# RWKV attention on TensorE tiles of 64: weights of 48 columns instead of 64 in three products, with the PSUM rows between zeroed once

## The chip, the cores and the metric

The kernel runs on one core of a Trainium2 chip. The metric is the device time of the core in microseconds. Three runs of the kernel before took 606.13, 604.15 and 604.02 us; the median is 604.15.

The engines are named as the profile names them: PE is TensorE's product, PEld its load of the stationary operand (the weights), DVE is VectorE, ACT is ScalarE, POOL is GpSimd, and SP issues most transfers.

## The reference

An RWKV attention over batch 4, 8 heads, 768 steps and head size 48 feeds a dense block with 3072 tokens, 384 inputs and 2048 hidden units, all in float32.

```python
for t in range(S):
    cur = einsum('bhd,bhe->bhde', u * k[t], v[t])
    y[t] = einsum('bhd,bhde->bhe', r[t], state + cur)
    state = w * state + einsum('bhd,bhe->bhde', k[t], v[t])
x = y.transpose(0, 2, 1, 3).reshape(B * S, H * D)
h = x @ w_in
out = (h - tanh(h)) @ w_out
```

## The kernel before

The attention is done in chunks. A unit, of which there are 24, is one chunk of `SHORT` = 64 steps for two of the four batches: `z` counts the batch in the unit, and the two batches lie in partitions 0 to 63 and 64 to 127. Heads come in pairs: `p` counts the four pairs and `i` the head of a pair. A head has 48 numbers, but in the padded tiles each head has `PAD` = 64 places, of which the last 16 hold zeros (`padded`, L533). `HEAD[i]` is the 48 used partitions that begin at 64 i, and `HALF[z]` the 64 of a batch.

In one unit TensorE does these steps, all through `put` (L696, which the profile records as L697) except the transpositions:

- `turn` (L740, recorded as L742) transposes `r` and `k` of the unit, 128 by 128.
- `from_state` (L786) multiplies the scaled `r` with the state from earlier chunks, into `y_ps`. The weights are the state, 48 rows by 64 columns, and 64 steps move. It is left out in the first chunk.
- `levels` (L797) makes the scores of the 64 steps among themselves; VectorE then copies the masked part of them over `at` (recorded at L896).
- `outputs` (L809) multiplies the scores with `v` and adds the result to `y_ps`. The weights are `v`, 64 rows by 64 columns.
- `to_state` (L823) makes the new state's product into `kv_ps`. The weights are the scaled `k`, 64 rows by 64 columns, and the 48 columns of `v` move. It is left out in the last chunk.

Each of `from_state`, `outputs` and `to_state` has 16 puts, four over each of the four 64x64 tiles of the array[...]. A float32 product leaves two loads and two products in the trace, so a call has 32 records of each.

In units 0 and 1 (`direct`, where the block of the output `j` is 0) `outputs` has 12 puts on `v` and 12 on `extra`, which holds the last two heads split over columns 48 to 63.

`y_ps` and `kv_ps` are parts of one PSUM tile of two banks, `yk_ps` (L558). ScalarE copies `y_ps` to `xt` and `rest` (`to_xt` L842, `to_rest` L847), all 64 rows of a head with them; afterwards GpSimd's small transfers (`fill`, recorded as L854) write the last two heads from `rest` into rows 48 to 63 of `xt`. VectorE adds `kv_ps` to the state over all 128 partitions (`keep`, L857) and then multiplies by the decay. From unit 16 on (`two`) the transposed `r` and `k` and the scores stand in `yk_ps` as well.

The dense block (`Dense`) works on tiles of 256 hidden units by 256 tokens: the first product (L167), five activations on ScalarE, four operations on VectorE, and the second product (L205, or L255 with seven products in place of eight).

The order of the work on every engine comes from `Plan` (L299). Each piece of work is added with an engine, a cost written as a constant, what it comes after and a due time; `order` (L442) lays it out with these and many random variations, and the instructions are then issued in that order. Work that is issued directly, such as the memsets at the top of `near` (L494), is not part of the plan and stands ahead of it. At the start `w` and `u` come as eight rows, which are transposed into `cols_ps`, eight columns of `yk_ps`.

Of the kernel before, what the change touches and what calls it, by code (L numbers as in the profile page):

```python
# [11 lines left out]
F32 = mybir.dt.float32  # L12
# [20 lines left out]
PAD = 64  # L33
# [460 lines left out]
def near(ctx, tc, r, k, v, w, u, out, shared, moe_w_in, moe_w_out):  # L494
# [3 lines left out]
    V, A, T, G, Q = nc.vector, nc.scalar, nc.tensor, nc.gpsimd, nc.sync  # L498
    d = shared["dims"]
    H, D, NP, NK, B, HEAD = d.H, d.D, d.NP, d.NK, d.B, d.HEAD  # L500
# [6 lines left out]
    ps_a = ctx.enter_context(tc.tile_pool(name="n_ps_a", bufs=1, space=PSUM))  # L507
# [4 lines left out]
    def fixed(name, shape, dt=F32):  # L512
        return const.tile(shape, dt, name=name, tag=name)
# [6 lines left out]
    HALF = [slice(z * SHORT, (z + 1) * SHORT) for z in range(2)]  # L520


    rows = fixed("rows", [2 * NP, 2, PAD])
    V.memset(rows, 1.0)
    same = fixed("same", [128, SHORT])
# [3 lines left out]
    V.memset(by[:, :, 0:1], 0.0)  # L529
    V.memset(plus, 0.0)  # L530
    V.memset(plus[:, :, 0:1], 1.0)

    def padded(name, count, new=fixed):  # L533

        tiles = [new(f"{name}{i}", [128, H, PAD]) for i in range(count)]
        for t in tiles:
            G.memset(t[:, :, D:], 0.0)
        return tiles
# [16 lines left out]
    before = before.bitcast(I32)[:, None, None, :].to_broadcast([128, 2, NP, SHORT])  # L555


    yk_ps = ps_a.tile([128, 2, 512], F32, name="yk_ps", tag="yk_ps")  # L558
    banks_now = [ExitStack(), ExitStack()]

    def banks(at, name, shapes):
# [34 lines left out]
    y_ps = yk_ps[:, :, :256].rearrange("e z (p t) -> e z p t", p=NP)  # L596
    kv_ps = yk_ps[:, :, 256 : 256 + NP * D].rearrange("d z (p e) -> d z p e", p=NP)
# [98 lines left out]
    def put(*args, **how):  # L696
        T.matmul(*args, skip_group_check=True, **how)  # L697
# [3 lines left out]
    def unit(n):  # L701
# [6 lines left out]
        t = SimpleNamespace(at=ats[n % 2])  # L708
        rt, vt, kw, state = rts[n % (AHEAD + 1)], vts[n % (AHEAD + 1)], kws[n % 2], states[half]
# [13 lines left out]
        direct = j == 0  # L723

        def fetch(name, src, after):
            def run(z):
                if name == "k" and not hasattr(t, "kt"):
                    t.kt = first_k[slot] if direct else load.tile([128, H, D], F32, name="kt", tag="kt")
                to = {"r": rt, "v": vt}.get(name)
                Q.dma_start(out=(t.kt if to is None else to)[HALF[z], :, :D],  # L730
                            in_=src[half * 2 + z, :, steps_at, :].rearrange("h t d -> t h d"))

            of = [add("SP", .65, lambda z=z: run(z), after, data=.71) for z in range(2)]
            return add("none", 0, lambda: None, of)
# [5 lines left out]
        def turn(src, to):  # L740
            for p in range(NP):
                T.transpose(to[:, p * C : (p + 1) * C], src[:, 2 * p : 2 * p + 2, :].rearrange("t h d -> t (h d)"), ident)  # L742
# [34 lines left out]
                    for i in range(2):  # L777
                        put(own_lev[HALF[z], i, p], t.kU[HEAD[i], p, z], t.rT[HEAD[i], p, z], start=True, stop=True)

        def to(i, z):  # L780


            i = i ^ z if swap else i
            return slice(i * PAD, (i + 1) * PAD)

        def from_state():  # L786
            for p in range(NP if ch else 0):
                for z in range(2):
                    for i in range(2):
                        put(y_ps[to(i, z), z, p], state[HEAD[i], z, p], t.rT[HEAD[i], p, z],  # L790
                            start=p == 0, stop=False)

        def between():
# [3 lines left out]
        def levels():  # L797
            if not two:
                from_state()
            for p in range(NP):  # L800
                for z in range(2):
                    for i in range(2):
                        put(lev[HALF[z], i, p], t.kT[HEAD[i], p, z], t.rT[HEAD[i], p, z], start=not two, stop=True)
# [3 lines left out]
            G.tensor_copy(extra[slot][:, :, :, D:], vt[:, 2 * NK :, :D].rearrange("s i (k x) -> s i k x", k=NK))  # L807

        def outputs():  # L809
            for p in range(NP - direct):  # L810
                for i in range(2):
                    for z in range(2):
                        put(y_ps[to(i, z), z, p], vt[HALF[z], 2 * p + i], t.at[HALF[z], i, p],
                            start=p == 0 and not ch, stop=p == NP - 1)
            for p in range(NK if direct else 0):
                for i in range(2):
                    for z in range(2):
                        put(y_ps[to(i, z), z, p], extra[slot][HALF[z], i, p], t.at[HALF[z], i, NK],
                            start=False, stop=p == NK - 1)
            if not direct:  # L820
                to_state()

        def to_state():  # L823
            for p in range(NP if more else 0):
                for i in range(2):
                    for z in range(2):
                        put(kv_ps[i * PAD : (i + 1) * PAD, z, p], kw[HALF[z], 2 * p + i], vt[HALF[z], 2 * p + i, :D],
                            start=p == 0 or not two, stop=True)

        def given(out, y):  # L830
# [60 lines left out]
        if two:  # L891
            now = add("PE", .68, from_state, both + [x.rT, b1.xt, b1.rest, b1.add, b2.decay, x.kT], steps=64)
            begun = [add("ACT", .15, between, [now])]
        x.lev = add("PE", .7 if two else (1.35 if swap else 1.75) if ch else .7, levels,
                    begun + [x.kT, x.rT, b2.out] + ([b2.decay, b1.xt, b1.rest, b1.add] if ch else []), steps=128 if ch and not two else 64)
        x.cp = add("DVE", .64, lambda: V.copy_predicated(t.at, before, lev), [x.lev, b2.out] + ([] if product else [x.diag]))  # L896
        x.out = now = add("PE", .95 if direct else 1.3, outputs,
                          [x.cp, x.diag, x.v, b1.xt, b1.rest, b1.add] + ([x.extra] if direct else [x.kw]), steps=96 if direct else 128)
        if direct:
            now = x.out = add("PE", .6, to_state, [now, x.kw], steps=64)  # L900
# [364 lines left out]
def kernel(  # L1265
# [29 lines left out]
    with tc.manual_schedule():  # L1295
        near(tc, r, k, v, w, u, out, shared, moe_w_in, moe_w_out)
# [39 lines left out]
```

## Time and profile before

| | us |
|---|---|
| median of three runs | 604.15 |
| the profiled execution, as timed | 606.31 |
| its span in the trace | 604.5 |
| PE busy | 583.7 |
| DVE busy | 466.9 |
| ACT busy | 403.6 |
| POOL busy | 204.6 |
| L697 alone, PE busy, 0 to 40 us | 8.77 |
| L697 alone, PE busy, 40 to 230 us | 27.71 |
| L697 alone, PE busy, 230 to 340 us | 0 |
| L697 alone, PE busy, 340 to 545 us | 20.54 |

A row of a group gives the line, the engine, the operation, output<-inputs by name, for PE the rows*columns of the weights, the shape of the moving operand, and the count; then the busy time, the mean length of one in ns, the idle time before it and what ended that. A row in order of time gives start and length in us first. A row of one tile or line gives least, median and longest duration in ns, then the first and last start. Products overlap on PE, and the ends of the products are modelled, so the lengths of single ones don't add up to the time they take together. The mean clock that TensorE was granted over the span was 0.993 of full speed.

### The profile page before, as it was taken

The numbers are of one execution on the slowest core, as the hardware profiler recorded it, in microseconds if no ns is written. First come the engines' busy times: TensorE is split into PE (matmuls) and PEld (weight loads), VectorE is DVE, ScalarE is ACT, GpSimd is POOL, SyncE is SP. The second block draws the span as 40 slices with busy tenths as digits, with TensorE's granted clock in tenths as the row PEclk, the third lists the DMA queues.
The fourth block names the chain that finished last, engine by engine and source line by source line (L and its number), as shares of the span: only waits on it lengthen the run. The fifth ranks groups of instructions, "written<-read, shape, count | busy, mean of one in ns | idle before, by whom it ended". The sixth has DMA issues, their size and how long they took to land.

```text
span 604.5 us, 14282 instructions
## 1 busy us (share of the span) xinstructions
PE 583.7 (97%) x5597; PEld 493.8 (82%) x5597; DVE 466.9 (77%) x775; ACT 403.6 (67%) x902; POOL 204.6 (34%) x372
## 2 busy tenths in 40 slices
PE   7889998999999999999999999999999999999994
PEld 5556776777777689899999999888989988899993
DVE  5789989999999999987667856756986665744753
ACT  3677988899986575656666655757784757665551
POOL 5001222301000244554455443432552434453531
PEclk9989999999999999999999999999999999999998
DMA  6986569572621210111011120131310100100101
GB/s 125 185 160 116 97 120 217 112 159 73 125 60 19 48 28 11 30 26 27 2 27 27 29 44 1 35 57 26 65 25 11 41 1 9 27 7 3 26 2 31
DMA packets 86325, 33.77 MB, mean 56 GB/s; under 512 B 78536, under 2 KB 80680, under 8 KB 86248
## 3 DMA queue, kind: packets, MB, share of 16 engines
q1 hardware_dynamic: 81084, 25.57, 21.5%
q0 software_dynamic: 4992, 6.99, 5.2%
q8 instruction: 46, 0.75, 0.6%
q14 instruction: 31, 0.25, 0.1%
q10 hardware_dynamic: 172, 0.20, 0.1%
HBM read 26.94 MB, written 4.72 MB: 52 GB/s over the span
## 4 chain that ended last, share of the span: by engine, by line
PE 81%; DVE 8%; ACT 5%; issue 2%; SPq 1%; DMA 1%; POOL 0%; ACTq 0%; DVEq 0%; POOLq 0%
PE h L167 38%; PE p L255 25%; PE o L205 9%; PE yk_ps L697 6%; DMA st<-in_moe_w_in_dram 1%; PE x_ps L742 1%; DVE rT L746 1%; SPq L730 1%; ACT kT L755 1%; PE yk_ps L742 1%; DVE tg L193 1%; PE x_ps L697 1%; ACT xt L833 1%; ACT s L176 1%; DVE tg L195 1%
## 5 line engine op out<-in xcount | busy, mean ns | idle before, releaser
L167 PE MATMUL h<-xt,w_in_sb 128*128 128x256 f32 x1152 | 283.8, 383 | 2.9 <-issue 1.6
L167 PEld LDWEIGHTS h<-xt,w_in_sb 128*128 128x128 f32 x1152 | 213.7, 191 | 33.8 <-issue 3.0
L240 POOL TENSOR_TENSOR sg<-g 128x256 f32<-128x256 f32 x71 | 54.8, 772 | 178.4 <-DVE g L197 149.7
L191 DVE TENSOR_TENSOR g<-h,th 128x512 f32<-128x512 f32 x96 | 66.0, 688 | 50.8 <-ACT s L176 24.0
L255 PE MATMUL p<-mixed,sg 128*128 128x192 f32 x426 | 104.1, 326 | 0.2 <-issue 0.2
L193 DVE SCALAR_TENSOR_TENSOR tg<-s,tg 128x512 f32<-128x512 f32 x96 | 69.5, 724 | 30.7 <-ACT tg L180 16.9
L178 ACT ACTIVATE th<-h 128x512 f32<-128x512 f32 x96 | 57.4, 597 | 51.8 <-PE h L167 51.8
L180 ACT ACTIVATE tg<-h 128x512 f32<-128x512 f32 x96 | 57.1, 595 | 42.6 <-PE h L167 42.5
L176 ACT ACTIVATE s<-h 128x512 f32<-128x512 f32 x96 | 57.4, 598 | 41.1 <-PE h L167 40.8
L854 POOL DMA_DIRECT2D xt<-rest x66 | 32.2, 494 | 148.4 <-ACT rest L833 147.6
L255 PEld LDWEIGHTS p<-mixed,sg 128*128 128x128 f32 x426 | 75.0, 190 | 0.4 <-issue 0.4
L197 DVE COPY_PREDICATED g<-small,tg 128x512 f32<-128x512 int32 x96 | 71.7, 747 | 4.5
L255 PE MATMUL p<-w_out_sb,g 128*128 128x192 f32 x284 | 70.7, 331 | 0.1
L195 DVE SCALAR_TENSOR_TENSOR tg<-q,tg 128x512 f32<-128x512 f32 x96 | 67.2, 700 | 4.1 <-DVE tg L193 0.5
L182 ACT ACTIVATE q<-s,m1b 128x512 f32<-128x512 f32 x96 | 69.7, 726 | 0.7
L184 ACT ACTIVATE small<-s,smallb 128x512 f32<-128x512 f32 x96 | 69.5, 724 | 0.4
L205 PE MATMUL o<-w_out_sb,g 128*128 128x384 f32 x192 | 69.6, 488 | 0.0
L255 PEld LDWEIGHTS p<-w_out_sb,g 128*128 128x128 f32 x284 | 52.0, 190 | 7.4 <-DVE e L283 0.5
L767 ACT ACTIVATE at<-same,du 128x64 f32<-128x64 f32 x184 | 48.0, 340 | 6.8 <-DVE du L763 6.4
L205 PEld LDWEIGHTS o<-w_out_sb,g 128*128 128x128 f32 x192 | 35.6, 190 | 15.8 <-DVE part L218 0.3
L244 POOL TENSOR_TENSOR sg<-sg,g 128x128 f32<-128x128 f32 x71 | 40.7, 573 | 5.1
L242 POOL TENSOR_TENSOR sg<-sg,g 128x128 f32<-128x128 f32 x71 | 38.8, 547 | 5.4
(129 smaller groups left out, 695.1 us busy)
## 6 DMA issues: line engine op xcount, KB each, us to landing
st<-in_moe_w_out_dram SPq DMA_DIRECT2D x8, 768.0 KB, 6.9
rt<-in_r_dram SPq DMA_DIRECT2D x48, 96.0 KB, 3.1
vt<-in_v_dram SPq DMA_DIRECT2D x48, 96.0 KB, 3.0
st<-in_moe_w_in_dram SPq DMA_DIRECT2D x16, 288.0 KB, 6.0
kt<-in_k_dram SPq DMA_DIRECT2D x44, 96.0 KB, 3.3
out_dram<-o POOLq DMA_DIRECT2D x44, 96.0 KB, 2.1
st<-in_moe_w_in_dram POOLq DMA_DIRECT2D x16, 96.0 KB, 3.7
xt<-rest POOLq DMA_DIRECT2D x66, 16.0 KB, 2.4
```

The source lines that it names most:

```text
L167: self.nc.tensor.matmul(t.h2[:, z], self.w_in_sb[:, t.f // 2, kk, z * 128 : (z + 1) * 128], self.xts[t.j][:, kk].rearrange("p b t -> p (b ...
L176: A.activation(out, t.h, AF.Square)
L178: A.activation(out, t.h, AF.Tanh)
L180: A.activation(out, t.h, AF.Tanh, scale=G1)
L182: A.activation(out, t.s, AF.Square, bias=self.m1b)
L184: A.activation(out, t.s, AF.Relu, bias=self.smallb, scale=-1.0)
L191: V.tensor_tensor(t.g, t.h, t.th, ALU.subtract)
L193: V.scalar_tensor_tensor(t.tg, t.s, C4, t.tg, ALU.mult, ALU.mult)
L195: V.scalar_tensor_tensor(t.tg, t.q, K1, t.tg, ALU.add, ALU.mult)
L197: V.copy_predicated(t.g, t.small.bitcast(I32), t.tg)
L205: self.nc.tensor.matmul(self.outs[i], t.g2[:, z, i * C : (i + 1) * C], self.w_out_sb[:, t.f + z, :], start=t.first and z == 0, stop=t.last ...
L255: self.nc.tensor.matmul(ps[bank][:, half * n : (half + 1) * n], a, b, start=t.first and half == 0, stop=t.last, skip_group_check=True)
```

## The change

Three products take 48 columns of weights in place of 64, so they write 48 rows of PSUM in place of 64: `from_state` (the state's 48 columns), `outputs` outside units 0 and 1 (48 columns of `v`), and `to_state` (48 columns of the scaled `k`). The function `to` gets the number of rows as a parameter. `yk_ps` is made earlier, and VectorE writes it once with zeros, so that rows 48 to 63 and 112 to 127, which these products no longer write, hold something defined where ScalarE and VectorE read them.

```diff
+    yk_ps = ps_a.tile([128, 2, 512], F32, name="yk_ps", tag="yk_ps")
     rows = fixed("rows", [2 * NP, 2, PAD])
...
     V.memset(plus[:, :, 0:1], 1.0)
+    V.memset(yk_ps, 0.0)
...
-    yk_ps = ps_a.tile([128, 2, 512], F32, name="yk_ps", tag="yk_ps")
...
-        def to(i, z):
+        def to(i, z, n=PAD):
             i = i ^ z if swap else i
-            return slice(i * PAD, (i + 1) * PAD)
+            return slice(i * PAD, i * PAD + n)
...
-                        put(y_ps[to(i, z), z, p], state[HEAD[i], z, p], t.rT[HEAD[i], p, z],
+                        put(y_ps[to(i, z, D), z, p], state[HEAD[i], z, p, :D], t.rT[HEAD[i], p, z],
...
         def outputs():
+            n = PAD if direct else D
...
-                        put(y_ps[to(i, z), z, p], vt[HALF[z], 2 * p + i], t.at[HALF[z], i, p],
+                        put(y_ps[to(i, z, n), z, p], vt[HALF[z], 2 * p + i, :n], t.at[HALF[z], i, p],
...
-                        put(kv_ps[i * PAD : (i + 1) * PAD, z, p], kw[HALF[z], 2 * p + i], vt[HALF[z], 2 * p + i, :D],
+                        put(kv_ps[HEAD[i], z, p], kw[HALF[z], 2 * p + i, :D], vt[HALF[z], 2 * p + i, :D],
```

## The prediction

> **What bounds the kernel now.** I read the page's first and fourth parts, then the groups of line 697 by shape, then the first 22 us and one late attention step in order of time, and the chain through that step.
>
> ```profile
> span 604.5 us, 14282 instructions
> PE 583.7 (97%) x5597; PEld 493.8 (82%) x5597; DVE 466.9 (77%) x775; ACT 403.6 (67%) x902; POOL 204.6 (34%) x372
> PE 81%; DVE 8%; ACT 5%; issue 2%; SPq 1%; DMA 1%; POOL 0%; ACTq 0%; DVEq 0%; POOLq 0%
> ...
> L697 PE MATMUL yk_ps<-at,vt 64*64 64x64 f32 x752 | 16.4, 224 | 2.0 <-DVE at L896 1.3 <-DVE at L883 0.7
> L697 PE MATMUL yk_ps<-rT,state 48*64 48x64 f32 x704 | 15.3, 224 | 4.1 <-DVE state L860 3.2 <-DVE rT L746 0.4 <-ACT kT L755 0.3
> L697 PE MATMUL yk_ps<-vt,kw 64*64 64x48 f32 x704 | 14.0, 217 | 0.0
> ```
>
> TensorE is busy 97% of the span and holds 81% of the chain that ended last. The change touches only the three groups shown (752, 704 and 704 records). A record is half of a float32 product: each `put` leaves two LDWEIGHTS and two MATMUL records, so one call of `to_state` is 16 puts and 32 records. "64*64" is rows times columns of the weights, the next pair is the moving operand. The busy time of a group is no guide to its price, because four tiles of the array run at once; the price has to be read from one stretch in order of time:
>
> ```profile
> 389.44 0.56 PEld L697 LDWEIGHTS yk_ps<-at,vt 64*64 64x64 f32 x32 [0.74 <-DVE at L896]
> ...
> 389.90 0.56 PEld L697 LDWEIGHTS yk_ps<-vt,kw 64*64 64x64 f32 x32
> ...
> 389.44 0.69 PE L697 MATMUL yk_ps<-at,vt 64*64 64x64 f32 x32 [0.34 <-DVE at L896]
> 389.96 0.63 PE L697 MATMUL yk_ps<-vt,kw 64*64 64x48 f32 x32
> 390.52 0.59 PE L255 MATMUL p<-w_out_sb,g 128*128 128x192 f32 x2
> ```
>
> ```profile
> 389.44 1.15 PE yk_ps L697 x64
> 390.59 1.50 PE p L255 x8
> ```
>
> The second fence is the chain in the same stretch: `outputs` and `to_state` run back to back on it, and the dense product queued behind starts as soon as they drain. So time saved in these groups should move the end, as long as nothing else is late.
>
> Within a call the 32 records go in 8 rounds of four, one round over the four 64x64 tiles. The records' own starts show four starts 6.7 ns apart and then the next round 58.3 ns after the last. Check it on the row: 32 loads take 0.56 us, one load is 0.135 us, so first to last start is 0.425 us; less 3 x 6.7 ns that leaves 0.405 for 7 rounds, 58 ns each.
>
> **What sets a round, and what 48 columns do to it.**
>
> ```profile
> L657 PEld LDWEIGHTS h<-one,ok x2: 80/80/81, 11.4 to 11.4; 128*1 128x1 f32 x2
> L657 PE MATMUL h<-one,ok x2: 163/163/163, 11.4 to 11.4; 128*1 128x1 f32 x2
> ...
> L697 PEld LDWEIGHTS yk_ps<-vt,kw x704: 129/135/135, 14.8 to 498.7; 64*64 64x64 f32 x176
> L697 PE MATMUL yk_ps<-vt,kw x704: 205/218/253, 14.8 to 498.7; 64*64 64x48 f32 x176
> ...
> L167 PEld LDWEIGHTS h<-xt,w_in_sb 128*128 128x128 f32 x1152 | 213.7, 191 | 33.8 <-issue 3.0
> ```
>
> A load of 1, 64 and 128 columns takes 80, 135 and 191 ns: 0.86 ns for each column over a fixed 80. A product with 64 moving columns takes 218, with 48 it takes 205 where it waits for nothing: 0.83 ns for each. So a load of 64 columns and a product of 64 both occupy a tile for about 53 ns, and the round of 58 ns is the longer of the two with some 5 ns added; they overlap, or a round would be 110.
>
> 1. `to_state`, 22 calls. It already moves 48 columns, yet its rounds last 58 ns and its later products 218 ns, 13 ns more than the first ones: they wait for weights of 64 columns. The one round that finds its weights loaded lasts 45 ns. With 48 columns the load also gives 58.3 - 16 x 0.83 = 45 ns. Seven rounds by 13.3 ns is 93 ns a call (the eighth overlaps the call before), 22 x 0.093 = 2.05 us.
>
> 2. `from_state` (22 calls) and `outputs` (22 of its 24; the first two keep 64 columns). The moving operand stays at 64, so a round stays at 58 ns whatever the load takes. Only the first load of a call that follows a 128-wide product lies open, 16 x 0.83 = 13 ns: 44 x 0.013 = 0.58 us. From below: nothing, if that load is not what opens the round. From above: if the 5 ns over 53 belong to the load, rounds fall to 53 and add 44 calls x 7 x 5 ns = 1.5 us. I take 0.58, since the row of `to_state`'s one loaded round (45 = 40 + 5) puts the 5 ns with the product.
>
> 3. The new memset, 128x1024 of PSUM on VectorE, once.
>
> ```profile
> 1.74 0.28 DVE L530 MEMSET plus<- 128x260 f32 x1
> 2.09 0.06 DVE L531 MEMSET plus<- 128x4 f32 x1
> ...
> 5.23 0.27 PE L640 MATMUL yk_ps<-ident,rows 8*128 8x8 f32 x1
> ...
> 5.74 0.42 DVE L643 TENSOR_SCALAR by<-yk_ps 128x256 f32<-128x256 f32 x1 [3.59 <-ACT saved L654]
> ```
>
> By the 0.28 us for 260 elements, 1024 take 1.1 us: from 2.15 to 3.25. VectorE idles 3.59 us there before L643. The transposition at L640 must now come after the memset, but it starts at 5.23, waiting for the two small loads of `rows`; ScalarE and all else follow it. Cover left is 2.0 us, so the cost is 0; it would be felt only if the memset took over 3.1 us, nearly three times the row.
>
> 4. Moved: nothing. The planner's costs are untouched, so every engine's queue and every DMA keeps its order; the memset is the only added instruction, and no wait is added but the memset's own. `yk_ps` is allocated earlier, with the same shape.
>
> Sum on TensorE: 2.05 + 0.58 = 2.63 us. What reaches the end: the first three calls of `to_state` (14.8, 22.6, 31.8 us) lie before a stop of 2.22 us in which TensorE waits for VectorE's state at L860, in a stretch where DMA and VectorE lead; I leave out their 0.28 us and that of the calls beside them, 0.05. From 38 us on the chain shows `outputs` with `to_state` as one piece of about 1.1 us again and again, and waits of TensorE after 40 us are few and below 0.45 us, but for one of 1.57 at 100.2 us in which it waits for nothing the profile shows. Those short waits end at VectorE (L896, L860) or ScalarE (kT), whose work starts from earlier products, so most of the saving passes through; for the part that a wait swallows I take off another 0.3. 2.63 - 0.33 - 0.3 = 2.0 us.
>
> The profiled execution took 606.31 us, 604.5 of span and 1.81 around it; its sum is 604.3. It is 2.16 us above the median of the runs shown, 604.15, but close to the slowest (606.13); the wait of 1.57 us at 100.2 may be most of that. None of the calls changed differs in it, so the same 2.0 comes off the median: 602.15, 0.33% less. About 0.5%, 3 us, is what a measurement of this kernel can tell from no change, so this lands in "same".
>
> **A rule against the change.** The Trainium skill, TensorEngine Tiling (Array Packing), section Instruction Overhead, says that each matmul carries some 60 cycles of overhead and one of free size 1 lasts as long as one of 60, so little is to be had from a dimension that is already small. By it shrinking 64 to 48 saves only the 4 above 60 instead of 16, a quarter of my sum: 0.5 us, 603.65. The row: products of 1, 48 and 64 columns take 163, 205 and 218 ns, and four tiles start 6.7 ns apart. The measurement decides: length grows with the columns below 60 too. What the trace has no row for is a load of 48.
>
> **The rivals.**
>
> No gain. A load of 48 columns costs as much as one of 64, as if columns were counted in strips of 32; or the short waits give the gain back. For it: the Trainium skill's TensorE: Matmul & The Clock Gate, Terms, has column groups as masks of 32. Against: one column took 80 ns where a strip of 32 would give 107. Time 603.7 to 604.6.
>
> More gain. The rounds of `outputs` and `from_state` are paced by the load's 5 ns too, and nothing is swallowed: 2.63 + 1.5 = 4.1 off, 600.0; half of that added part gives 600.8. For it: both kinds of round have the same 58.3. Against: the 45 ns round.
>
> Slower. A 48-column load, which ends in the middle of the tile's second strip, no longer overlaps the tile's own product. The round is then load plus product: 40 + 53 + 5 = 98 for `outputs` and `from_state`, 40 + 40 + 5 = 85 for `to_state`; 44 x 8 x 40 ns + 22 x 8 x 27 ns = 14.1 + 4.8 = 18.9 us, 623. It ends beyond 0.5% as soon as 6 ns a round are lost and nothing is won: 66 x 8 x 6 ns = 3.2 us. Against: rows of 48 (`48*64`) already run at the same round as 64, and a load of one column shows no penalty; but all overlapping tiles in this trace have 64 columns.
>
> **How the numbers follow.** My forecast, 601.2 to 603.2: 0.55. No gain or a small loss, 603.2 to 606: 0.18; a run with a stop like that at 100.2 falls here as well. More gain, below 601.1: 0.15. Slower, above 607.2: 0.12. Faster 0.15, same 0.73, slower 0.12. The range leaves out the 0.12 above and about 0.08 of the low tail: 600.5 to 605.8.
>
> **What would show it.** Right: loads of the three groups at about 121 ns, `to_state`'s products at 205, its call down from 0.63 to about 0.54 us; `outputs` still 0.69 or 0.68; the memset about 1.1 us, ended by 3.4, and L640 still at 5.2. Wrong: loads of 48 still at 135 (no gain); calls of `outputs` near 0.65 (more gain); calls longer than 0.75 us, or products that no longer start while the next load runs (slower); L640 later than 5.5 (the memset is not covered). The step I trust least is that 48 columns are loaded like 64 less a quarter.

## The result, and the profile after

In 22 runs beside 22 of the kernel before, the medians are 602.38 and 604.65 us; the ratio is 0.9961, with a 95% interval of 0.9948 to 0.9974. That is 0.39% or 2.4 us faster, 1.6 to 3.1 by the interval. The forecast was 2.0 us, 602.15. By the bound of 0.5% set there it counts as "same", though the interval excludes no change. Of the runs whose granted clock is on record, those at 0.995 and more and those below it lie some 1.7 us apart in either kernel (medians 604.0 and 605.8 before, 601.7 and 603.5 after), and the change is worth 2.3 us in both groups.

The page of the kernel after: span, busy time, and the chain that ended last by engine.

```profile
span 600.9 us, 14283 instructions
PE 580.2 (97%) x5597; PEld 489.9 (82%) x5597; DVE 466.9 (78%) x776; ACT 403.6 (67%) x902; POOL 204.7 (34%) x372
PE 78%; DVE 8%; ACT 6%; SPq 3%; issue 2%; DMA 1%; POOL 1%; ACTq 0%; DVEq 0%; POOLq 0%
```

TensorE is busy for 3.5 us less, with as many records as before. The spans of the two profiled executions differ by 3.6 us, which is more than the runs do. In this one TensorE also came to its full clock earlier, so that everything from 5 us on stands 0.4 us ahead (see the start below), and a stop of TensorE near 100 us was 0.6 shorter.

The groups of the line, which is now L698, by shape. A row of a line or a tile shows least, median and longest duration in ns.

```profile
L698 PEld LDWEIGHTS yk_ps<-at,vt x752: 116/120/135, 12.9 to 535.1; 64*48 64x48 f32 x176, 64*64 64x64 f32 x12
L698 PE MATMUL yk_ps<-at,vt x752: 216/216/267, 12.9 to 535.2; 64*48 64x64 f32 x176, 64*64 64x64 f32 x12
L698 PEld LDWEIGHTS yk_ps<-vt,kw x704: 116/122/122, 14.3 to 495.4; 64*48 64x48 f32 x176
L698 PE MATMUL yk_ps<-vt,kw x704: 202/205/241, 14.3 to 495.4; 64*48 64x48 f32 x176
```

A load of 48 columns takes 120 to 122 ns, as extrapolated (121), and `to_state`'s products have come down from 218 to 205, so they no longer wait for their weights. The products of `outputs` are down too, from 218 to 216, and this is where the working of the forecast is off.

The same attention step as before the change, in order of time and then as a piece of the chain:

```profile
386.84 0.66 PE L698 MATMUL yk_ps<-at,vt 64*48 64x64 f32 x32 [0.36 <-DVE at L898]
387.33 0.54 PE L698 MATMUL yk_ps<-vt,kw 64*48 64x48 f32 x32
387.79 0.59 PE L255 MATMUL p<-w_out_sb,g 128*128 128x192 f32 x2
```

```profile
386.84 1.02 PE yk_ps L698 x64
387.86 1.50 PE p L255 x8
```

From the start of `outputs` to the dense product behind `to_state` it took 1.08 us (389.44 to 390.52), and it takes 0.95 now. `to_state` went from 0.63 to 0.54, as announced. `outputs` went from 0.69 to 0.66, which was not: the prediction expected 0.69 or 0.68, and named 0.65 as a sign of more gain. The rounds follow from these rows. For `to_state`, 0.54 less the last product's 0.205 and less 3 x 6.7 ns leaves 0.315 for 7 rounds, 45 ns each. For `outputs`, 0.66 less 0.216 and the same 20 ns leaves 0.424; by the records' own starts the first round takes 93 of it and each of the six others 55.8 (58.3 before).

The start, with the new memset:

```profile
2.36 0.91 DVE L533 MEMSET yk_ps<- 128x1024 f32 x1 [0.21 <-issue]
...
4.85 0.22 PE L641 MATMUL yk_ps<-ident,rows 8*128 8x8 f32 x1
...
5.31 0.42 DVE L644 TENSOR_SCALAR by<-yk_ps 128x256 f32<-128x256 f32 x1 [2.04 <-ACT saved L655]
```

The memset ends at 3.27 us, 1.6 us ahead of the transposition, which did not become later. That it came 0.4 us earlier (5.23 before) is not the change. TensorE's wait for the two loads of `rows` ends at 3.5 us in both traces; the transposition then still stands in the queue behind filling products (L632, now L633). Such a product with 256 moving columns takes 634 ns until the record of the granted clock begins, at 5.43 us before and at 4.40 after, and 380 ns from then on. In the other traces with one memset it is the same: where the record begins after 5.23 us, the transposition starts at 5.23 or 5.24, and where it begins at 4.50 and 4.95, at 4.90 and 5.12.

Since TensorE's order is the same in both kernels, each of its 5597 products can be set beside the one in the other trace. From 110 us on the distance between the two traces moves only in small steps: -0.096 us behind every call of `to_state`, -0.031 behind every call of `from_state` and `outputs`. That is 22 x 0.096 + 44 x 0.031 = 3.48 us, close to the 3.5 of the busy time. Against them stand a few steps back where TensorE waits for others. From 110 us to the end the steps forward sum to 1.86 us and those back to 0.44. Between 29 and 63 us the calls save 0.63 us but the distance grows by 0.22 only; from 45 to 63 us alone they save 0.32 and the distance grows by 0.01. Half of that is lost at 60.2 us, where `outputs` waits for VectorE's copy (L896, now L898): its loads waited 0.34 us before and wait 0.50 now.

### The profile page after: what moved, and what is told of

The parts are those of the page before. It is cut to its first block, busy times and chain, and to the rows that moved or that the text cites. A ratio compares the mean times of both kernels' runs of the same rounds, so it can differ in the third digit from the quotient of the medians.

```text
span 600.9 us, 14283 instructions
## 1 busy us (share of the span) xinstructions
PE 580.2 (97%) x5597; PEld 489.9 (82%) x5597; DVE 466.9 (78%) x776; ACT 403.6 (67%) x902; POOL 204.7 (34%) x372
## 4 chain that ended last, share of the span: by engine, by line
PE 78%; DVE 8%; ACT 6%; SPq 3%; issue 2%; DMA 1%; POOL 1%; ACTq 0%; DVEq 0%; POOLq 0%
PE h L167 37%; PE p L255 25%; PE o L205 8%; PE yk_ps L698 5%; SPq L731 3%; DVE rT L747 1%; ACT kT L756 1%; PE x_ps L743 1%; PE yk_ps L743 1%; DMA kt<-in_k_dram 1%; DVE tg L193 1%; ACT s L176 1%; ACT xt L835 1%; DVE g L191 1%; ACT tg L180 1%
## 5 line engine op out<-in xcount | busy, mean ns | idle before, releaser
L167 PE MATMUL h<-xt,w_in_sb 128*128 128x256 f32 x1152 | 283.5, 383 | 1.8 <-PE x_ps L698 1.0
L167 PEld LDWEIGHTS h<-xt,w_in_sb 128*128 128x128 f32 x1152 | 213.5, 191 | 32.7 <-ACT xt L835 1.0
```

The lines of the kernel that those rows point to most:

```text
L167: self.nc.tensor.matmul(t.h2[:, z], self.w_in_sb[:, t.f // 2, kk, z * 128 : (z + 1) * 128], self.xts[t.j][:, kk].rearrange("p b t -> p (b ...
```

## The experiments

**One part alone.** Three kernels undo the rest of the change: `to_state` alone, the two products into `y_ps` alone, and neither.

```diff
# to_state alone, against the changed kernel
-    put(y_ps[to(i, z, D), z, p], state[HEAD[i], z, p, :D], t.rT[HEAD[i], p, z],
+    put(y_ps[to(i, z), z, p], state[HEAD[i], z, p], t.rT[HEAD[i], p, z],
...
-            n = PAD if direct else D
+            n = PAD
# from_state and outputs alone
-    put(kv_ps[HEAD[i], z, p], kw[HALF[z], 2 * p + i, :D], vt[HALF[z], 2 * p + i, :D],
+    put(kv_ps[i * PAD : (i + 1) * PAD, z, p], kw[HALF[z], 2 * p + i], vt[HALF[z], 2 * p + i, :D],
# memset alone: both of these
```

> The change with to_state alone at 48 columns of weights; from_state and outputs keep 64; the memset stays. Theory (a round of the four tiles lasts as long as the longer of load and product, plus a few ns): to_state's rounds fall from 58 to 45 ns, its 22 calls by 95 ns each, 2.1 us of TensorE's busy time; some two thirds reach the end, 1.4 us, ratio 0.9977. from_state and outputs keep rounds of 58. Rival (the time comes from elsewhere, the start or the stops of TensorE): the calls shorten, and the ratio stays within 0.001 of 1.

> The change with from_state and outputs alone at 48 columns; to_state keeps 64; the memset stays. Theory: a call is 13 ns shorter by its first load and some 15 ns by rounds of 55.8 in place of 58.3 ns, 44 calls by 30 ns = 1.3 us of TensorE, some 0.9 us at the end, ratio 0.9985. By the prediction's own step only the first load counts: 0.58 us of TensorE, 0.4 at the end, rounds still 58.3. Rival (strips of 32 columns): nothing, ratio 1.

> All three products at 64 columns as before; only the memset and the earlier allocation of yk_ps are kept. Theory: the memset ends near 3.3 us, under the wait for the first small transfers, and costs nothing: ratio 1 within 0.001, spans and groups of line 698 as before. Rival (the gain came with the memset or the allocation, or the memset costs what the products gain): a ratio off 1 by more than 0.0015 one way or the other.

| | median, us | ratio to before | 95% interval |
|---|---|---|---|
| `to_state` alone | 603.17 | 0.9977 | 0.9962 to 0.9992 |
| `from_state`, `outputs` alone | 604.03 | 0.9986 | 0.9975 to 0.9996 |
| memset alone | 604.24 | 0.9999 | 0.9988 to 1.0011 |
| before, in these runs | 604.47 | | |

The parts add up: 0.23% and 0.14% make 0.37%, against 0.39% for the whole, and the memset with the earlier allocation does nothing that shows. So the gain is the products'. The rows of the line in the kernel with `to_state` alone, then in the one with the other two:

```profile
L698 PEld LDWEIGHTS yk_ps<-at,vt x752: 129/135/135, 13.3 to 538.5; 64*64 64x64 f32 x188
L698 PE MATMUL yk_ps<-at,vt x752: 218/218/268, 13.3 to 538.6; 64*64 64x64 f32 x188
L698 PEld LDWEIGHTS yk_ps<-vt,kw x704: 116/122/122, 14.8 to 498.6; 64*48 64x48 f32 x176
L698 PE MATMUL yk_ps<-vt,kw x704: 202/205/240, 14.8 to 498.7; 64*48 64x48 f32 x176
```

```profile
L698 PEld LDWEIGHTS yk_ps<-at,vt x752: 116/120/135, 12.9 to 536.5; 64*48 64x48 f32 x176, 64*64 64x64 f32 x12
L698 PE MATMUL yk_ps<-at,vt x752: 216/216/268, 12.9 to 536.6; 64*48 64x64 f32 x176, 64*64 64x64 f32 x12
L698 PEld LDWEIGHTS yk_ps<-vt,kw x704: 129/135/135, 14.4 to 496.7; 64*64 64x64 f32 x176
L698 PE MATMUL yk_ps<-vt,kw x704: 205/218/253, 14.4 to 496.8; 64*64 64x48 f32 x176
```

Each product's own load decides over its own time: 205 or 218 for 48 moving columns, 216 or 218 for 64. By the records' own starts `to_state`'s rounds are 45 ns in the first kernel and 58.3 in the second; those of `outputs` are 58.3 and 55.8. The prediction's step for `outputs`, rounds that stay at 58, is refuted here: they fall by 2.5.

**Which of the two sets a round.** First fewer weights still, then fewer moving columns. Both kernels leave out a part of the result and are there for their time alone.

```diff
# 40 columns of weights in all three
-            n = PAD if direct else D
+            n = PAD if direct else 40
...
-    put(kv_ps[HEAD[i], z, p], kw[HALF[z], 2 * p + i, :D], vt[HALF[z], 2 * p + i, :D],
+    put(kv_ps[i * PAD : i * PAD + 40, z, p], kw[HALF[z], 2 * p + i, :40], vt[HALF[z], 2 * p + i, :D],
# (from_state likewise)
# 48 moving steps in outputs
-    put(y_ps[to(i, z, n), z, p], vt[HALF[z], 2 * p + i, :n], t.at[HALF[z], i, p],
+    put(y_ps[to(i, z, n), z, p, : n if not direct else SHORT], vt[HALF[z], 2 * p + i, :n],
+        t.at[HALF[z], i, p, : n if not direct else SHORT],
```

> As the changed kernel, but with 40 columns of weights in the three products, so 8 of 48 rows of the attention's outputs and of the state's products are left out; it is there for the time alone. Theory: loads take 114 ns; from_state and outputs stay at rounds of 55.8, since their 64 moving columns set them, and lose 7 ns in the first load; to_state stays near 43 to 45, since its 48 moving columns now set it. TensorE gains 0.3 to 0.6 us over the changed kernel, ratio 0.995 to 0.9965. Rival 1 (the load sets every round): to_state at 38 ns and the others below 52, 1.0 + 1.2 us more, ratio below 0.9935. Rival 2 (columns are counted in strips of 32, or cost only at the end): loads of 120 ns and no difference at all.

> As the changed kernel, but outputs moves 48 of the 64 steps outside units 0 and 1, so the last 16 steps of each chunk get no share of the scores' product; it is there for the time alone. Theory (a round is the longer of load + 5 ns and product + 2.5 ns): with 48 columns and 48 steps a call of outputs has rounds of 45 ns in place of 55.8 and starts its products over 0.37 us in place of 0.448; with the last product 13 ns shorter that is 0.09 us a call, 22 calls 2.0 us less of TensorE than the changed kernel; two thirds to all of it at the end, 1.3 to 2.0 us, ratio 0.993 to 0.994. Rival (rounds under 56 ns in outputs are held by something other than the moving columns): rounds stay at 55.8 and the ratio at 0.996.

Measured with 40 columns: 601.66 us, 0.9961 (0.9946 to 0.9977), no different from the changed kernel's 0.9961. With 48 steps: 601.11 us, 0.9942 (0.9927 to 0.9958), beside 601.96 for the changed kernel in the same runs. The line with 40 columns, then with 48 steps:

```profile
L698 PEld LDWEIGHTS yk_ps<-at,vt x752: 109/113/135, 13.3 to 534.4; 64*40 64x40 f32 x176, 64*64 64x64 f32 x12
L698 PE MATMUL yk_ps<-at,vt x752: 216/216/267, 13.3 to 534.4; 64*40 64x64 f32 x176, 64*64 64x64 f32 x12
L698 PEld LDWEIGHTS yk_ps<-vt,kw x704: 109/113/113, 14.8 to 494.6; 64*40 64x40 f32 x176
L698 PE MATMUL yk_ps<-vt,kw x704: 202/203/233, 14.8 to 494.6; 64*40 64x48 f32 x176
```

```profile
L698 PEld LDWEIGHTS yk_ps<-at,vt x752: 115/122/136, 13.3 to 534.0; 64*48 64x48 f32 x176, 64*64 64x64 f32 x12
L698 PE MATMUL yk_ps<-at,vt x752: 204/206/268, 13.3 to 534.1; 64*48 64x48 f32 x176, 64*64 64x64 f32 x12
```

The load falls by another 7 ns with 40 columns, so columns are not counted in strips of 32. But `outputs` keeps 216 ns and rounds of 55.8; `to_state` goes from 45 to 42.5 and no further, since its 48 moving columns hold it. With 48 moving columns `outputs` gets rounds of 45, and a call's products start over 0.37 us as expected. Of the 2.0 us (22 x 0.09) that TensorE saves by this, 0.85 reach the end by the medians of the same runs and 1.3 by the ratios to before, whose intervals overlap. All these rounds follow one rule, at 0.833 ns a column, which is the slope between a load-bound round at 64 and one at 48:

| kernel, call | columns loaded | columns moving | load + 5 | product + 2.5 | round measured, ns |
|---|---|---|---|---|---|
| before, `outputs` | 64 | 64 | 58.3 | 55.8 | 58.3 |
| before, `to_state` | 64 | 48 | 58.3 | 42.5 | 58.3 |
| after, `outputs` | 48 | 64 | 45 | 55.8 | 55.8 |
| after, `to_state` | 48 | 48 | 45 | 42.5 | 45 |
| 40 columns, `outputs` | 40 | 64 | 38.3 | 55.8 | 55.8 |
| 40 columns, `to_state` | 40 | 48 | 38.3 | 42.5 | 42.5 |
| 48 steps, `outputs` | 48 | 48 | 45 | 42.5 | 45 |

The rule's constants are fitted: 0.833 and 5 come from the rounds of 58.3 and 45, and 2.5 from those of 55.8 and 42.5. What the rows test is that the longer of the two sets the round. The last row was expected by the rule before it ran.

**How much cover the memset had.**

```diff
-    V.memset(yk_ps, 0.0)
+    for _ in range(4):
+        V.memset(yk_ps, 0.0)
```

> As the changed kernel, with the memset of yk_ps written four times over. Theory: one takes 0.91 us, so four end near 6.0 us instead of 3.27; the transposition of w and u starts near 6.1 in place of 4.85 to 5.23, 0.9 to 1.2 us late, and the chain of small steps behind it as well; at the end 0.3 to 1.1 us later than the changed kernel, ratio 0.9965 to 0.998. Rival (the wait on the memset is covered by something longer, or the start doesn't reach the end): ratio 0.996 as the changed kernel.

Measured: 604.99 us, 1.0003 (0.9989 to 1.0018), so four memsets cost 2.4 us against the changed kernel's 0.9963 in the same runs (3.0 by the medians): the whole gain, and more than twice the 0.3 to 1.1 expected. The start of that kernel, then the same products before the change:

```profile
4.76 0.91 DVE L534 MEMSET yk_ps<- 128x1024 f32 x1 [0.29 <-DVE yk_ps L534]
5.96 0.91 DVE L534 MEMSET yk_ps<- 128x1024 f32 x1 [0.29 <-DVE yk_ps L534]
6.93 0.27 PE L642 MATMUL yk_ps<-ident,rows 8*128 8x8 f32 x1 [1.62 <-DVE yk_ps L534]
...
9.00 1.06 PE L744 MATMUL x_ps<-ident,first_k 128*128 128x128 f32 x4
...
12.14 0.60 PE L629 MATMUL h<-ident,twice 128*128 128x128 f32 x4
```

```profile
6.40 0.60 PE L742 MATMUL x_ps<-ident,first_k 128*128 128x128 f32 x4
...
9.42 0.66 PE L627 MATMUL h<-ident,twice 128*128 128x128 f32 x4 [0.69 <-ACT twice L651]
```

Each memset waits 0.29 us for the one before, which was not expected, so the last ends at 6.87. The transposition starts 1.7 us later than at 5.23, and TensorE stands still for 1.62 us in front of it. Behind it the delay grows: the table of decays (L629) is 2.7 us late (12.14 against 9.42). Between the two stand the same filling products and the first transpositions, in the fixed order of the queue, and they last longer here, as the row of `first_k` shows (1.06 us in place of 0.60). The record of the granted clock begins at 10.96 us in this trace and between 4.40 and 7.06 in the eleven others, and until it begins a filling product with 256 moving columns lasts 634 ns in place of 380. TensorE's work between the transposition and the table so takes 1.7 us longer than before the change, and the wait of 0.69 us in front of the table takes up only a part of that. The stop is the likely reason for the late clock, since no other trace has one there; it is one trace, so this is a lean. The step "cost 0" stands for one memset, which is covered; of what sticks out past the cover the runs show nothing absorbed.

**A new order for the shorter pieces.** The planner's costs are lowered to what the trace shows.

```diff
-    x.lev = add("PE", .7 if two else (1.35 if swap else 1.75) if ch else .7, levels,
+    x.lev = add("PE", .7 if two else (1.32 if swap else 1.72) if ch else .7, levels,
-    x.out = now = add("PE", .95 if direct else 1.3, outputs,
+    x.out = now = add("PE", .95 if direct else 1.17, outputs,
# from_state .68 to .65, to_state .6 to .5
```

> As the changed kernel, with the planner's costs of the changed pieces lowered to what the trace shows: to_state .6 to .5, outputs with it 1.3 to 1.17, from_state .68 to .65, levels with from_state 1.35 to 1.32. The planner then finds another order. Theory: the sum of work is the same, so the end moves by how well the waits after 40 us are filled; 1 us either way, ratio 0.9945 to 0.998. If the saving that waits swallow (about 1 us) is lost because the order was laid for the longer pieces, the new order wins it back: 0.994 to 0.995.

> The changed kernel once more, on the chip of these runs, for the comparison with them: ratio 0.996.

The new order gives 603.10 us, 0.9975 (0.9962 to 0.9989); the changed kernel in the same runs 601.96, 0.9963 (0.9948 to 0.9977). So shorter costs did not win back what the waits swallow. TensorE's busy time is 580.5 and 580.9 in their profiles, so its work is the same. The order found is no better; it has waits of its own, such as one of 1.35 us for VectorE's copy (L898) at 92.8 us, and whether the costs or the luck of the search made it so was not tried. No other kernel with the whole result was clearly faster than the changed one.

**Where the saving is swallowed.** TensorE gains 3.5 us, the runs 2.4. The change is made in the first six units alone, and in the others alone.

```diff
         direct = j == 0
+        cols = D if n < 6 else PAD     # the other kernel: n >= 6
# cols in place of D in the three products
```

> The change in units 0 to 5 alone (up to about 61 us); from unit 6 on all three products keep 64 columns. TensorE saves 6 x 96 + 8 x 31 ns = 0.82 us. Theory (up to some 65 us VectorE, ScalarE and transfers lead, and waits swallow most of it): 0.1 to 0.35 us at the end, ratio 0.9994 to 1. Rival (TensorE leads there too, or a share of two thirds passes everywhere): 0.55 to 0.8 us, ratio 0.9987 to 0.9991.

> The change in units 6 to 23 alone; the first six units keep 64 columns. TensorE saves 16 x 96 + 36 x 31 ns = 2.65 us. Theory: waits after 65 us swallow some 0.4 to 0.6 of it, 2.0 to 2.3 us reach the end, ratio 0.9962 to 0.9967, about that of the whole change. Rival (two thirds pass everywhere): 1.75 us, ratio 0.9971.

Measured: the early units 604.49 us, 0.9994 (0.9980 to 1.0008); the late ones 601.93, 0.9955 (0.9936 to 0.9974); before 604.93 in these runs. The late units alone have the gain of the whole change, the early ones none that shows. Both intervals still touch the rival's values, so by the runs alone this is a lean. The steps between the traces say the same (0.22 of 0.63 us gets through between 29 and 63 us, all of it from there to 98 us), but they come from one pair of traces.

## Why the prediction was right

- *TensorE bounds it, and a saving in these calls moves the end.* Right from some 65 us on: behind each call the traces part by what the call saves, less 0.44 us of steps back after 110 us.
- *Step 1, `to_state`, 93 ns a call, 2.05 us.* Right: 96 ns, 2.1 us. The 48-column load takes 120 to 122 ns.
- *Step 2, `from_state` and `outputs`, 13 ns a call, 0.58 us.* The first load lies open as said; the first round went from 107 to 93 ns. But the choice between the two ends was wrong: "the row of `to_state`'s one loaded round (45 = 40 + 5) puts the 5 ns with the product". A product adds 2.5 and a load 5, so each of the later rounds fell by 2.5 as well, and a call saves 31 ns: 44 x 0.031 = 1.36 us, between the 0.58 and the 2.1 (0.58 + 1.5) that the prediction gave as its ends. The one round that I read as a product's was a start ahead of the weights: its products last 218 ns, 13 ns longer than those of the first round, so they waited, and the loads' own starts are 58 ns apart there as everywhere in the call.
- *Step 3, the memset at no cost.* Right: 0.91 us in place of 1.1, ended at 3.27; the kernel with it alone is at 0.9999. But the transposition did not start at 5.23 because of the loads of `rows`, as I read it: TensorE's wait for them ends at 3.49, and what stands ahead of it then are filling products, the last of them from 4.67 to 5.30.
- *Step 4, nothing is moved.* Right: every engine's order is the same but for the memset.
- *What reaches the end.* Off the other way. I took 0.63 us off; some 1.1 are swallowed (3.48 less the 2.4 of the runs), 0.44 of it after 110 us and most of the rest before 65. The boundary set at 38 us was too early, since between 45 and 63 us next to nothing gets through, half of it lost at a wait for VectorE. The two errors partly cancel: 3.48 - 1.1 = 2.4 in place of 2.63 - 0.63 = 2.0. That the total is off by no more than 0.4 us is in part luck.
- *The profiled execution before.* I put most of its 2.16 us above the median down to the stop at 100.2 us. The clock is the likelier reason: from 39.6 to 43.0 us the granted clock was 0.50 in it, and half of that stretch, 1.7 us, is the distance between the two groups of runs. With 40 columns the profiled execution has a longer stop, 2.1 us, and no such stretch, and took 601.92 us, 0.26 above its kernel's median.
- *The rule against the change.* It would have allowed a quarter, 0.5 us. As quoted there it speaks of the free size, the moving side, while the change shortens the weights, so it bore on this case only by likeness. Products of 48 and 64 columns take 205 and 218 ns, and rounds of loads of 48 and 64 differ by 13; the measurement decides against it on both sides.
- *The rivals.* No gain by strips of 32 is ruled out by loads of 113 and 120 ns. More gain was half right: the rounds of `outputs` and `from_state` did fall, by 2.5 ns and not by 5, but waits took more than the forecast allowed, not nothing. The slower case, loads that no longer overlap, would have shown rounds of 85 ns and more; in the changed calls none is above 56 but the first.

## What to carry to other kernels

Where small products run on several tiles at once, read the time from the spacing of rounds, not from the busy time of the group: in these kernels it is the longer of load and product, and only the longer one is worth shortening. Here padded weights cost their full width where fewer columns move than are loaded. Where as many move, the padding cost 2.5 ns a round and 13 ns in the first load of a call. An addition ahead of a fixed order costs nothing while the engine behind it is held up anyway; what stuck out here reached the end.

## What was not expected of the hardware

- In rounds over four 64x64 tiles a load-bound round is its columns at 0.833 ns and 5 ns (58.3 for 64, 45 for 48), a product-bound one its columns and 2.5 ns (55.8 and 42.5). A tile gets one load and one product in each round; at 0.833 ns a column these are 53.3 ns each for 64 columns, and the round takes 58.3, so by this estimate a load overlaps the product that runs on its own tile.
- The clock that TensorE is granted changes within an execution. Besides the end of the kernel, it is 0.50 for one or two stretches of 3.41 us in 8 of the 12 traces (from 39.6 to 43.0 us in the kernel of before), and a first product of the dense block (L167) lasts 631 ns in one and 379 behind it. The four traces without a stretch have a mean clock of 0.996 or 0.997, the seven with one 0.992 to 0.995, the one with two 0.990. What sets them off was not tried.
- Two memsets of VectorE to the same PSUM tile stand 0.29 us apart, though nothing else lies between; one of 128x1024 zeros takes 0.91 us.
- In 11 of the 12 profiled executions TensorE stops near 100 us, in front of a first product (L167), for 0.7 to 2.1 us while nothing that the profile shows holds it. In the kernel of before:

```profile
99.69 0.47 PE L697 MATMUL x_ps<-rT,kT 48*64 48x64 f32 x20
101.73 0.38 PE L167 MATMUL h<-xt,w_in_sb 128*128 128x256 f32 x1 [1.57 <-issue]
```

In the kernel with the new order it is not there. Its lengths differ by 1.4 us among these executions, more than half of the gain. The traces point to the fetching of instructions. In all eleven the stop ends in front of the same product, and 2.4 to 2.7 us behind the start of a transfer of 16 KB that the profile calls "instruction" (in the kernel of before, 99.17 us and 101.73):

```profile
q8 instruction: 46, 0.75, 0.6%
```

There are 46 such transfers for TensorE's 11,312 instructions in the kernel of before, one for some 246. That TensorE waits for them there was not tried, and stays open.
